# Routing tables and expert weights in attention with a top-1 expert layer: limits read from PSUM, weight splits moved, three first products ahead

## The chip, the cores and the metric

The kernel runs on one core of a Trainium2 chip. The metric is the device time of one execution in microseconds (us). A core has TensorE (matrix products into PSUM), VectorE, ScalarE, GpSimd and SyncE (SP, which here only issues DMAs); the profile calls them PE, DVE, ACT, POOL and SP. PEld is TensorE's loading of weights. Line numbers (L681) are those of the kernel before.

## What is computed

The reference takes q, k and v of 8 batches, 8 heads, 576 rows and 64 columns, and does thresholded attention followed by a layer of 8 experts of which each token uses one:

```python
scores = scale * np.matmul(q, k.transpose(0, 1, 3, 2))
thresh = np.max(scores, axis=-1, keepdims=True) - tau
scores = np.where(scores >= thresh, scores, -1000000000.0)
attn = softmax(scores)                       # over the last axis
x = (attn @ v) laid out as 4608 tokens x 512
expert_idx = np.argmax(x @ w_gate, axis=1)   # gate_w: its softmax probability
for e in range(8):
    mask = expert_idx == e
    h = np.maximum(x[mask] @ w1[e], 0.0)     # 512 -> 1024
    out[mask] = gate_w[mask, None] * (h @ w2[e])
```

All in float32. The kernel keeps that precision by splitting each value into a high and a low float16 half and adding three products (high by high, high by low, low by high).

## The kernel before

**Order of the work.** The kernel is written as a list of steps k. A pair is two heads; there are 32 pairs (NPAIR) of 11 steps each (NSTEP), four pairs to a batch. In the step loop (L1178 to L1211) a pair's scores are made first to find row maxima (`s_unit`, L345), then, ten steps later, made again transposed with the threshold subtracted (`st_unit`, L398): ScalarE takes the exponential (L421), VectorE the mask (L424), ScalarE casts to float16 (L429, the high half) and GpSimd subtracts (L430, the low half; two pieces of the last pair are VectorE's). `av_piece` (L447) multiplies both halves with v, for which `split_v` (L282) and `low_part` (L248) prepare v's halves: ScalarE casts, TensorE puts the cast into a PSUM bank with an identity product (L254), VectorE subtracts (L255). Other work is put into steps with `plan(k, f)` and `after(k, f)`; `hurry(f)` runs f, and all that f plans, with preference. KEND = 352 is the step at which the last pair's scores are done.

Within the emitted program a scheduler orders each engine's instructions by readiness in its own timing model, earlier emitted ones first. `keep_in_program_order` pins an instruction behind what was emitted before it on its engine, and preference ranks it ahead. Each engine, and each DMA queue, then runs its list in order.

**Routing.** When a batch's attention is done, `finish` (L504) scales it, sends the rows through SP's transposes (L543), and `logits` (L551) and `route` (L576) pick each token's expert and its place. `send` (L632) scatters the rows with GpSimd's indirect DMA to one DRAM area per expert (`xs`). Tables of row numbers are made three times, after batches 5, 6 and 7 (`tables0`, `tables1`, `tables2`, L1036 to L1051, through `level`, L1007): `counts` (L661) sums the tokens per expert on TensorE into a PSUM bank and subtracts each expert's base (L665) into the SBUF tile cnt; `table_first` (L668) makes lim = cnt - 1 (L681) and has = cnt > 0.5 (L689), both SBUF to SBUF, then the rows and the flags of rows past the limit, in the same PSUM bank (L682 to L691), and casts them to integers (L658). From table 0 the tiles 0 to 2 of expert 0 are gathered (`fetch`, L819: GpSimd indirect DMA L847, SP transpose L857, small operations L860 and L865), from table 1 tiles 3 to 6, from table 2 the others. A tile is 128 tokens.

**Experts.** `gemm1` (L878) multiplies a group's tokens with w1 on TensorE (L902), ScalarE and VectorE make the two halves of relu (L890, L891); `gemm2` (L914) multiplies with w2 (L935), ScalarE scales by the gate (L946), GpSimd scatters to the output (L949). Groups 0 to 7 are single tiles. `experts` (L1058) gives the order: first product of group i, then second product of group i - 1. Both come in chunks of 12 x 128 columns. Up to step 336 none is emitted, then 0.15 chunk a step, from 352 one chunk a step.

**Weights.** `load_w` (L786) loads a 512 KB quarter of w1 or w2 through SP, `split_w` (L801) makes its halves: ScalarE casts (L806), for expert 0 with the identity product and VectorE's subtraction (L255), pinned in program order, for others VectorE subtracts directly (L814). Expert 0 has two load buffers. Its eight splits, w1 then w2, stand at steps 318, 320, ..., 332 (L1085 to L1088), with the loads two ahead of them. The other experts' weights are due at chunks; 'close' (L1076) at step 364 opens their eight buffers.

Of the kernel before, what the change touches and what calls it, by code (L numbers as in the profile page):

```python
# [14 lines left out]
ALU = mybir.AluOpType  # L15
# [3 lines left out]
B, H, S, D = 8, 8, 576, 64  # L19
# [31 lines left out]
def kernel(  # L51
# [123 lines left out]
    def plan(k, f, where=END):  # L175
        if urgent[0]:
            f = hurry(f)
        assert (k, where) >= (now[0], slot[0])
        acts.setdefault(k, ([], [], []))[where].append(f)

    def hurry(f):

        def g():
            was, urgent[0] = urgent[0], True
            with tc.high_priority():
                f()
            urgent[0] = was

        return g
# [471 lines left out]
    def counts(nm):  # L661
        pc = ps_m.tile([P, 512], F32, tag="m", name=f"pc_{nm}")
        nc.tensor.matmul(pc[:, 0:E], ones, run, start=True, stop=True)
        c = tp.tile([P, E], F32, name=f"cnt_{nm}")
        nc.vector.tensor_tensor(c, pc[:, 0:E], base_e, ALU.subtract)  # L665
        return c, pc

    def table_first(nm, bank, cnt, start=None):  # L668

        bc = [P, E, NE]  # L670
        if start is None:
            rk_i = tp.tile(bc, I32, name="rk_i")
            nc.gpsimd.iota(rk_i, pattern=[[0, E], [P, NE]], base=0, channel_multiplier=1)
            nc.vector.tensor_copy(rk_f, rk_i)
        rk, bad = (bank[:, z:z + E * NE].rearrange("p (e n) -> p e n", e=E) for z in (32, 96))
        if start is None:
            nc.scalar.copy(rk, rk_f)
        else:
            nc.vector.tensor_tensor(rk, rk_f, start.unsqueeze(2).to_broadcast(bc), ALU.add)
        lim = tp.tile([P, E, 1], F32, name=f"lim{nm}")  # L680
        nc.vector.tensor_scalar(lim[:, :, 0], cnt, -1.0, None, ALU.add)  # L681
        nc.vector.tensor_tensor(bad, rk, lim.to_broadcast(bc), ALU.is_gt)  # L682
        nc.vector.tensor_scalar(bad, bad, float(1 << 20), None, ALU.mult)
        badi = to_int(bad, bc, f"badi{nm}")
        nc.vector.tensor_tensor(rk, rk, lim.to_broadcast(bc), ALU.min)
        nc.vector.tensor_tensor(rk, rk, base_e.unsqueeze(2).to_broadcast(bc), ALU.add)

        has = tp.tile([P, E, 1], F32, name=f"has{nm}")
        nc.vector.tensor_scalar(has[:, :, 0], cnt, 0.5, None, ALU.is_gt)  # L689
        nc.vector.scalar_tensor_tensor(rk, rk, pos0, has.to_broadcast(bc), ALU.subtract, ALU.mult)  # L690
        nc.vector.tensor_scalar(rk, rk, pos0, None, ALU.add)  # L691
        rowi = to_int(rk, bc, f"row{nm}")
        return rowi, badi
# [76 lines left out]
    groups += [(m, m + 1) for m in range(NPR, NEARLY, 2)]  # L770
    groups += [(m,) for m in range(NEARLY, NS)]
    group_of = {m: (g, i) for g in groups for i, m in enumerate(g)}
    ms = {}
    wq = {}
    T = {}
# [25 lines left out]
    def split_w(e, w, c):  # L801
        wf = wq.pop((e, w, c))

        o = (wb1, wb2)[w][0 if e == "x" else e % 2][:, c].rearrange("p (a h d) -> p a h d", a=w + 1, h=2)
        x = wf.rearrange("p (a d) -> p a d", a=w + 1)
        hi = nc.scalar.activation(o[:, :, 0], x, AF.Copy, scale=SW)  # L806
        if e == 0:
            tc.keep_in_program_order(hi)
            for i in range(2):
                t = slice(512 * i, 512 * i + 512)  # L810
                y = (x[:, i], o[:, i, 0], o[:, i, 1]) if w else (x[:, 0, t], o[:, 0, 0, t], o[:, 0, 1, t])
                after(2, lambda y=y, i=i: low_part(*y, SW, f"w{w}_{c}_{i}"), END if i else MID)
            return
        nc.vector.scalar_tensor_tensor(o[:, :, 1], x, SW, o[:, :, 0], ALU.mult, ALU.subtract)  # L814
# [59 lines left out]
    def chunks(g):  # L874

        return 8 * shape(g)[1] // P
# [180 lines left out]

    def experts():  # L1058

        for i in range(len(groups) + 1):  # L1060
            if i < len(groups):
                assert there(groups[i], 0)
                yield from gemm1(groups[i])
                past[0] = groups[i][-1]
            if i:
                assert there(groups[i - 1], 1)
                yield from gemm2(groups[i - 1])
                past[1] = groups[i - 1][-1]

    def room():  # L1070
        ldp.close()
# [11 lines left out]
    k = NSTEP * (NPAIR - 2) - LEAD - SL  # L1083
    plan(k + 1, room)
    for i in range(8):  # L1085
        plan(k + WS0 + WSD * i, lambda i=i: split_w(*wseq[i]))
        if i + 2 < 8:
            plan(k + WS0 + WSD * i, lambda i=i: load_w(*wseq[i + 2]))  # L1088
    TABLES = {B - 3: tables0, B - 2: tables1, B - 1: tables2}
    plan(KEND + 12, close)  # L1090


# [7 lines left out]

    at = []
    k = 0
    for i, g in enumerate(groups):
        at.append(k)
        k += chunks(g) + (chunks(groups[i - 1]) if i else 0)
    for i, g in enumerate(groups):
        for j, m in enumerate(g):
            if m >= NF + 2:
# [29 lines left out]
    def there(g, w):  # L1138

        e = g[0] // NE if g[0] < NEARLY else E + g[0] - NEARLY  # L1140
        return all((e, w, c) in split_done for c in range(4))
# [149 lines left out]
```

## Time and profile before

| | |
|---|---|
| median of 3 runs | 994.06 us (992.13 to 997.44) |
| profiled execution, its own time | 992.38 us |
| its span, first to last instruction | 990.7 us |
| mean granted TensorE clock | 0.987 of full speed |
| TensorE / VectorE / ScalarE / GpSimd busy | 95% / 71% / 66% / 57% of the span |

The profile is one execution. A timeline row gives the start and duration in us, the engine, the line, the operation, what it writes and reads, the size, a count where like instructions are merged, and in brackets how long the engine stood idle before it and what ended the idle time. A wait for several things is put down to the one that came last. Spans of GpSimd are rough, and ends of matrix products are modelled.

### The profile page before, as it was taken

What the parts mean: (1) busy time and instruction counts of PE and PEld (TensorE: products, weight loads), DVE (VectorE), ACT (ScalarE), POOL (GpSimd) and SP (SyncE); (2) the same over time, 40 slices, a digit from 0 to 9 for tenths busy, and PEclk for the clock granted to TensorE, in tenths of its full rate; (3) what the DMA queues carried; (4) which work ended last, traced back from release to release, by engine and by line L of the source; (5) the groups of instructions that cost most, each with busy time, mean ns of one, the idle gap of its engine ahead of it and who ended that gap; (6) DMA issues with size and microseconds to landing.
All of it is one profiled execution on the core that took longest, in us unless ns stands there. A gap on an engine that the chain in (4) does not pass through costs nothing. (4 is left out here: it accounts for less than half of the span.)

```text
span 990.7 us, 28651 instructions
## 1 busy us (share of the span) xinstructions
PE 939.0 (95%) x11548; PEld 604.1 (61%) x11548; DVE 702.8 (71%) x1413; ACT 652.3 (66%) x1111; POOL 561.6 (57%) x470
## 2 busy tenths in 40 slices
PE   7899999999999999999897898999999999999997
PEld 2355556556566556565564586777667766667684
DVE  7899999998999989999899875826243342423650
ACT  2689897997998889898988973534243342433651
POOL 6366886895996987978968871433122121221121
PEclk8899999999999999999999999999999999999999
DMA  6553554564564755646646639998574656556730
GB/s 199 143 132 80 146 134 125 140 164 112 127 179 115 162 125 141 171 94 170 152 97 188 149 104 289 363 228 250 164 232 115 216 151 180 171 155 209 224 105 27
DMA packets 142750, 159.20 MB, mean 161 GB/s; under 512 B 96403, under 2 KB 112789, under 8 KB 142614
## 3 DMA queue, kind: packets, MB, share of 16 engines
q1 hardware_dynamic: 126598, 100.33, 40.2%
q10 hardware_dynamic: 6768, 27.55, 8.9%
q0 software_dynamic: 9248, 29.45, 8.9%
q8 instruction: 92, 1.51, 0.7%
q14 instruction: 44, 0.36, 0.1%
HBM read 90.24 MB, written 19.44 MB: 111 GB/s over the span
## 5 line engine op out<-in xcount | busy, mean ns | idle before, releaser
L430 POOL TENSOR_TENSOR pl<-e,ph 128x1024 f16<-128x1024 f32 x158 | 335.9, 2134 | 105.1 <-ACT ph L429 66.6
L421 ACT ACTIVATE e<-st,ntau 128x512 f32<-128x512 f32 (+1 forms) x352 | 222.5, 650 | 54.2 <-PE st L405 51.5
L424 DVE SCALAR_TENSOR_TENSOR e<-st,e 128x512 f32<-128x512 f32 (+1 forms) x352 | 219.7, 635 | 12.2 <-ACT e L421 11.4
L935 PE MATMUL y<-wb,hl 128*128 128x512 f16 (+1 forms) x1056 | 201.8, 360 | 0.0
L368 DVE TENSOR_REDUCE nm<-s 128x1 f32<-128x512 f32 x300 | 188.1, 632 | 19.1 <-PE s L358 16.8
L902 PEld LDWEIGHTS <-wb 128*128 128x128 f16 x2304 | 188.2, 98 | 19.8 <-issue 1.2
L902 PE MATMUL h<-xTm,wb 128*128 128x256 f16 (+2 forms) x2112 | 195.2, 253 | 0.7 <-DMA xTm<-R 0.7
L474 PE MATMUL av<-vop,ph 128*128 128x65 f16 (+3 forms) x3072 | 187.7, 195 | 2.3 <-ACT x L484 2.0
L474 PEld LDWEIGHTS <-ph 128*128 128x128 f16 (+1 forms) x3072 | 158.3, 100 | 46.3 <-issue 21.3
L474 PE MATMUL av<-vop,pl 128*128 128x65 f16 (+1 forms) x1536 | 167.5, 194 | 4.6 <-POOL pl L430 4.5
L429 ACT CAST ph<-e 128x1024 f16<-128x1024 f32 x160 | 166.2, 1040 | 5.3 <-DVE e L424 5.0
L474 PEld LDWEIGHTS <-pl 128*128 128x128 f16 (+1 forms) x1536 | 136.6, 100 | 35.8 <-issue 10.5
L935 PEld LDWEIGHTS <-hl 128*128 128x128 f16 (+1 forms) x1056 | 94.0, 100 | 97.9 <-issue 1.9
L814 DVE SCALAR_TENSOR_TENSOR wb<-wf,wb 128x1024 f16<-128x1024 f32 x88 | 103.9, 1220 | 52.0 <-ACT wb L806 51.9
L404 PE MATMUL st<-QK 128*128 128x512 f16 (+3 forms) x640 | 138.8, 294 | 1.9 <-DVE lo L255 0.8
L405 PE MATMUL st<-CQ,ck 128*128 128x512 f16 (+3 forms) x640 | 137.4, 288 | 0.0
L356 PE MATMUL s<-QK 128*128 128x512 f16 (+1 forms) x600 | 129.6, 293 | 3.1 <-DMA QK<-hi 2.0
L358 PE MATMUL s<-ck,CQ 128*128 128x512 f16 (+1 forms) x600 | 128.0, 289 | 1.2 <-DMA CQ<-hi 1.2
L949 POOL DMA_INDIRECT out_dram<-o,gt x40 | 46.6, 1165 | 129.9 <-ACT o L946 118.8
L890 ACT ACTIVATE hl<-h 128x512 f16<-128x512 f32 (+1 forms) x80 | 45.6, 572 | 105.6 <-PE h L902 103.6
L806 ACT ACTIVATE wb<-wf 128x1024 f16<-128x1024 f32 x96 | 97.4, 1049 | 26.9 <-DMA wf<-in_w_dram 10.7
L860 DVE COPY gt<-R 128x1 f32<-128x1 f32 x33 | 5.1, 153 | 129.0 <-DMA out_dram<-o,gt 105.8
(194 smaller groups left out, 1016.6 us busy)
## 6 DMA issues: line engine op xcount, KB each, us to landing
wf<-in_w_dram SPq DMA_DIRECT2D x96, 512.0 KB
qkf<-in_qk_dram ACTq DMA_DIRECT2D x30, 576.0 KB
vf<-in_v_dram ACTq DMA_DIRECT2D x15, 640.0 KB
QK<-hi SPq DMA_DIRECT2D x64, 144.0 KB
QK<-lo SPq DMA_DIRECT2D x64, 72.0 KB
QK<-hi SPq DMA_DIRECT2D x64, 72.0 KB
ck<-lo SPq DMA_DIRECT2D x64, 72.0 KB
CQ<-hi SPq DMA_DIRECT2D x64, 64.0 KB
```

Of the source, the lines that this page charges most:

```text
L356: nc.tensor.matmul(sc[rows, oc], d["QA"][a][:, cols], d["KB"][a][:, CH[c]], start=True, stop=False)
L358: nc.tensor.matmul(sc[rows, oc], d["CQ"][:, at:at + cols.stop - cols.start], d["CK"][a][:, CH[c]], start=False, stop=True,)
L368: nc.vector.tensor_reduce(o, sc[:, 0:width(t)], axis=AX.X, op=ALU.max, negate=True)
L404: nc.tensor.matmul(sc[rows, oc], d["KB"][a][:, cols], d["QA"][a][:, CH[c]], start=True, stop=False)
L405: nc.tensor.matmul(sc[rows, oc], d["CK"][a][:, cols], d["CQ"][:, q], start=False, stop=True)
L421: nc.scalar.activation(pf, sc, AF.Exp, bias=ntau, scale=0.125 / SS)
L424: nc.vector.scalar_tensor_tensor(pf, sc, 0.0, pf, ALU.is_ge, ALU.mult)
L429: nc.scalar.copy(h, pd)
L430: (nc.vector if (n, t) in PLV else nc.gpsimd).tensor_tensor(l, pd, h, ALU.subtract)
L474: nc.tensor.matmul(av[:, 0:D] if z == 2 else av, l if z == 1 else h, vop[:, tv, W:W + D] if z == 2 else vop[:, tv, 0:W], start=i in (0, NT ...
L902: nc.tensor.matmul(o, Wt[:, c, wh, f], x, start=c == 0 and z == 0, stop=c == 3 and z == 2,)
L935: nc.tensor.matmul(o, h[:, hh], Wt[:, f, wh, c], start=f == 0 and z == 0, stop=f == 7 and z == 2)
```

## The change

`counts` writes the difference into the PSUM bank and copies it to SBUF with ScalarE; `table_first` reads the limit and the test from the bank. `experts` follows a list of turns, in which the first product of group 2 comes ahead of the second product of group 0; after that the order is as before. Expert 0's splits of w2 move from steps 326, 328, 330 and 332 to steps 353, 355, 357 and 359, those of w2 are no longer pinned in program order, and the loads of the last two quarters of w2 move along from steps 326 and 328 to 353 and 355. `tables0` is emitted with preference, and with it the gathers of tiles 0 to 2. The due chunks of later gathers follow from the new list (only group 5's differs, 25 instead of 33).

```diff
@@ counts
-        nc.vector.tensor_tensor(c, pc[:, 0:E], base_e, ALU.subtract)
+        nc.vector.tensor_tensor(pc[:, 8:8 + E], pc[:, 0:E], base_e, ALU.subtract)
+        nc.scalar.copy(c, pc[:, 8:8 + E])
@@ table_first
-        nc.vector.tensor_scalar(lim[:, :, 0], cnt, -1.0, None, ALU.add)
+        nc.vector.tensor_scalar(lim[:, :, 0], bank[:, 8:8 + E], -1.0, None, ALU.add)
...
-        nc.vector.tensor_scalar(has[:, :, 0], cnt, 0.5, None, ALU.is_gt)
+        nc.vector.tensor_scalar(has[:, :, 0], bank[:, 8:8 + E], 0.5, None, ALU.is_gt)
@@ after group_of
+    turns = [(1, 0), (1, 1), (1, 2), (0, 0), (0, 1), (1, 3), (0, 2)]
+    turns += [(w, i + w) for i in range(3, len(groups)) for w in (1, 0) if i + w < len(groups)]
@@ split_w
-        if e == 0:
+        if e == 0 and w == 0:
             tc.keep_in_program_order(hi)
...
@@ experts
-        for i in range(len(groups) + 1):
-            if i < len(groups):
-                assert there(groups[i], 0)
-                yield from gemm1(groups[i])
-                past[0] = groups[i][-1]
-            if i:
-                assert there(groups[i - 1], 1)
-                yield from gemm2(groups[i - 1])
-                past[1] = groups[i - 1][-1]
+        for first, i in turns:
+            assert there(groups[i], 1 - first)
+            yield from (gemm1 if first else gemm2)(groups[i])
+            past[1 - first] = groups[i][-1]
@@ the splits of expert 0
     for i in range(8):
-        plan(k + WS0 + WSD * i, lambda i=i: split_w(*wseq[i]))
+        t = k + WS0 + WSD * i if i < 4 else KEND + 1 + 2 * (i - 4)
+        plan(t, lambda i=i: split_w(*wseq[i]))
         if i + 2 < 8:
-            plan(k + WS0 + WSD * i, lambda i=i: load_w(*wseq[i + 2]))
-    TABLES = {B - 3: tables0, B - 2: tables1, B - 1: tables2}
+            plan(t, lambda i=i: load_w(*wseq[i + 2]))
+    TABLES = {B - 3: hurry(tables0), B - 2: tables1, B - 1: tables2}
@@ due chunks of the gathers
-    for i, g in enumerate(groups):
-        at.append(k)
-        k += chunks(g) + (chunks(groups[i - 1]) if i else 0)
+    for begin, i in turns:
+        if begin:
+            at.append(k)
+        k += chunks(groups[i])
```

## Rows read from the trace of the kernel before

**Rows 1.** Busy us by stretch: PE, PEld, DVE, ACT, POOL, then PEclk, DMA share, GB/s.
```profile
536.80:541.80 5.00, 1.02 (x6) 0.29 (x3) 5.00 (x5) 2.52 (x4) 4.83 (x4) 1.00 0.93 232
541.80:546.20 4.40, 4.36 (x13) 1.12 (x14) 4.40 (x10) 2.54 (x4) 2.72 (x4) 0.61 0.40 103
546.20:558.00 11.80, 7.38 (x103) 4.70 (x103) 10.73 (x26) 11.10 (x17) 11.11 (x8) 1.00 0.74 197
558.00:588.00 30.00, 30.00 (x686) 25.55 (x683) 21.90 (x57) 24.51 (x53) 22.69 (x18) 1.00 0.37 86
588.00:655.00 67.00, 63.45 (x748) 45.13 (x746) 43.66 (x113) 29.57 (x46) 24.23 (x26) 1.00 1.06 302
...
541.80:583.20 41.40, 36.94 (x671) 26.67 (x672) 33.63 (x76) 36.46 (x64) 35.54 (x28) 0.96 0.49 120
```

**Rows 2.** Timeline of VectorE: limit and test of table 0, limit of table 1.
```profile
536.80 4.29 DVE L681 TENSOR_SCALAR lim<-cnt 128x8 f32<-128x8 f32 x1
541.01 0.16 DVE L689 TENSOR_SCALAR has<-cnt 128x8 f32<-128x8 f32 x1
...
583.55 0.17 DVE L681 TENSOR_SCALAR lim<-cnt 128x8 f32<-128x8 f32 x1
...
584.89 0.20 DVE L683 TENSOR_SCALAR pc<-pc 128x32 f32<-128x32 f32 x1
```

**Rows 3.** Timeline of GpSimd at the same time.
```profile
536.71 2.28 POOL L536 TENSOR_TENSOR R<-xn,R 128x512 f16<-128x512 f32 x2
538.94 2.12 POOL L430 TENSOR_TENSOR pl<-e,ph 128x1024 f16<-128x1024 f32 x1
```

**Rows 4.** Timeline of TensorE, 537 to 558 us: its waits, and two like products.
```profile
537.44 0.38 PE L358 MATMUL s<-ck,CQ 128*128 128x512 f16 x1
541.82 0.77 PE L254 MATMUL hi_w<-wb,ident_h 128*128 128x512 f16 x2 [4.00 <-DVE nm L368]
...
543.84 0.63 PE L358 MATMUL s<-ck,CQ 128*128 128x512 f16 x1
...
550.42 0.59 PE L254 MATMUL hi_w<-wb,ident_h 128*128 128x512 f16 x2 [1.41 <-ACT wb L806]
...
553.57 0.59 PE L254 MATMUL hi_w<-wb,ident_h 128*128 128x512 f16 x2 [0.63 <-ACT wb L806]
...
557.41 0.44 PE L254 MATMUL hi_v<-vop,ident_h 128*128 128x320 f16 x2 [2.27 <-ACT vop L286]
```

**Rows 5.** ScalarE's groups, 543 to 581 us; one copy; the low halves' minimum/median/maximum (ns).
```profile
L421 ACT ACTIVATE e<-st,ntau 128x512 f32<-128x512 f32 (+1 forms) x25 | 15.5, 661 | 4.3 <-PE st L405 4.2
...
L806 ACT ACTIVATE wb<-wf 128x1024 f16<-128x1024 f32 x4 | 4.2, 1049 | 0.1
...
583.61 0.17 ACT L1020 COPY pc<-cnt 128x8 f32<-128x8 f32 x1 [0.89 <-DVE cnt L665]
...
L255 DVE SCALAR_TENSOR_TENSOR wb<-wf,hi_w x16: 665/675/687, 528.1 to 559.4; 128x512 f16<-128x512 f32 x16
```

**Rows 6.** GpSimd's groups, 541 to 583.3 us, and its last low half.
```profile
L430 POOL TENSOR_TENSOR pl<-e,ph 128x1024 f16<-128x1024 f32 x12 | 25.6, 2133 | 3.1 <-ACT ph L429 3.0
L633 POOL DMA_INDIRECT xs<-R,posi x4 | 4.3, 1071 | 0.8 <-issue 0.8
L847 POOL DMA_INDIRECT Rm<-xs,row x3 | 3.0, 983 | 1.9 <-DVE e L424 1.4 <-issue 0.3 <-PE av L474 0.2
...
581.04 2.13 POOL L430 TENSOR_TENSOR pl<-e,ph 128x1024 f16<-128x1024 f32 x1
```

**Rows 7.** Waits from 560 to 660 us (total, times, longest): ScalarE's for weights, SP's for gathers.
```profile
ACT wb L806 <- DMA wf<-in_w_dram: 10.1, 6, 3.7
...
SPq L857 <- DMA Rm<-xs,row: 4.1, 2, 3.7
```

**Rows 8.** Timeline of TensorE: a tile's first product, and tile 7's.
```profile
621.85 5.52 PE L902 MATMUL h<-spare,wb 128*128 128x128 f16 x96
...
654.81 5.52 PE L902 MATMUL h<-xTm,wb 128*128 128x128 f16 x96 [0.74 <-DMA xTm<-R]
```

## Prediction

> **What bounds the kernel now.** I read the page's busy shares first, then the busy time by stretches, then the timelines of the engines around the stretch that stands out. By stretches [rows 1], TensorE is all but gapless from 558 us on (30.00 of 30 us, 63.45 of 67), so whatever brings the work of this second part forward shortens the run, provided that its inputs come forward too. Just ahead of it lie three poor stretches: 1.02 busy of 5.0 us, then 4.4 us at a mean granted clock of 0.61, then 7.38 of 11.8.
>
> The cause of the first is one VectorE instruction. The limit of the first table, 128x8, takes 4.29 us at 536.80, while the same line takes 0.17 us at 583.55 [rows 2]. On GpSimd element-wise work runs back to back over just that time, from 536.71 to 541.06, and VectorE's next one starts at 541.01 [rows 2, 3]: VectorE waits until GpSimd falls free. TensorE waits 4.00 us behind it for a score bank, and a 512-column product then takes 0.63 us where it took 0.38 before: by the mean clock of 0.61 most of that stretch runs at 1.2 GHz instead of 2.4 [rows 1, 4]. The third stretch is ScalarE's: TensorE waits 1.41 and 0.63 us for splits of the second weights and 2.27 us for the split of v, which stands behind one of them on ScalarE [rows 4]; four such splits take 4.2 us there [rows 5].
>
> A rule of the Trainium skill bears on the first (SBUF — State Buffer, Who interferes with whom): a VectorE tensor_scalar with both ends in SBUF can take the port pair that it shares with GpSimd, the later of the two blocks until the first finishes, and a PSUM operand rules that mode out. The trace agrees on the block, not on its length: by the rule it ends with one GpSimd instruction, by the rows it lasted until GpSimd had none left, 4.29 us. If one instruction were the limit, the first term below would be about half.
>
> **The change part by part.** The sum is made against the profiled execution, 992.38 us; the median of the runs shown is 994.06, so 1.68 us is added at the end.
>
> *Limits from PSUM.* Subtraction, limit and test stay three small VectorE instructions per table. For a scalar operation that reads PSUM the nearest row is the table's own one of 0.20 us [rows 2]. That takes 4.1 us off VectorE, once; the other tables have nothing to lose. On TensorE it gives back the 4.00 us and, for the half-speed stretch, 4.4 x (1 - 0.61) = 1.7 us. A copy of 128x8 on ScalarE comes in three times, 0.17 us by the nearest copy [rows 5]. Bounds: nothing, or, in the last table, up to 3.7 us behind a weight split that waits for its load [rows 7]. I take nothing, since the limit no longer reads the copied value.
>
> *Second weights behind the last pair.* Four ScalarE splits (4.2 us), eight VectorE low halves of 0.68 us [rows 5], eight 512-column products and two 512 KB loads leave the time from 544 to 560 us. TensorE's three waits, 4.3 us, go at most. The work comes back some 20 to 30 us later, where ScalarE is busy 24.51 of 30 us and DMA only to 0.37 [rows 1]. Its cost there is between nothing, where ScalarE fills its idle time, and 3.7 us a split, the longest wait of one for its load [rows 7], with the exponentials and evacuations of the last pair queued behind it. I take nothing, because the row of DMA at 0.37 is the nearer one: the 3.7 us was seen at 1.06. On VectorE the low halves (8 x 0.68 = 5.4 us) stand ahead of the last batch's scaling at worst; 21.90 of 30 us are busy there. SP issues the two late loads as buffers fall free, ahead of the last batch's transposes, and passes none of them.
>
> *Three first products ahead.* The third tile's 96 products, 5.52 us a tile [rows 8], pass the first tile's second ones. The work is the same; TensorE gets 24 chunks of cover instead of 16 while the second weights arrive. Should that cover end early, the price is the wait above and a low clock after it. The gather of tile 5 comes due eight chunks sooner, at no cost: table 1 has its rows by then, and the next product to need it is as far off as before.
>
> *First table preferred.* Some twelve VectorE instructions of about 0.2 us come sooner, and with them three gathers, three SP transposes and the small copies on VectorE and GpSimd. No product waits for these tiles now, so nothing is gained. The gathers (0.98 us each) pass low halves on GpSimd, and one of them already stops that queue for 1.4 us [rows 6]: bounds 1.4 us gained and twice that lost. On SP the transposes can wait 3.7 us for gathered rows [rows 7], ahead of the last pair's thresholds; they stand there today too, so nothing.
>
> **The sum.** TensorE alone would come forward by 4.00 + 1.7 + 1.41 + 0.63 + 2.27 = 10.0 us. But the second part needs the last batch, and that needs the last pair's low halves from GpSimd. From 541.8 to 583.2 us GpSimd is busy 35.54 of 41.4; only ScalarE has more, 36.46, and it is to lose 4.2 [rows 1]. Of GpSimd's idle time 3.0 us stand ahead of low halves and 1.4 ahead of a gather; the rest are gaps of some 0.2 us ahead of gathers and sends [rows 6]. So its last low half, at 581.04, can come 4.4 us sooner. Three of the four sends of this stretch stand late, among the last low halves; at (4.3 + 0.8) / 4 = 1.3 us each they are another 3.8 us if all fall behind the last low half: 8.2. ScalarE allows 4.2 us of waits for TensorE and 4.2 of splits, 8.4 [rows 5]. I take the middle of 4.4 and 8.2, 6.3 us, because the sends' own inputs come forward as well, so that some will stay ahead. From there the last batch's chain is as before up to tile 7, for which TensorE already waits 0.74 us at 654.81 [rows 8]. So the chain hands its 6.3 us to the end, and what TensorE has beyond, 3.7 us, turns into a longer wait for that tile or for the last logits. 992.38 - 6.3 + 1.68 = 987.8 us, and 985.9 to 989.7 between the two ends.
>
> **The rivals.** *GpSimd is no limit*: all its sends move behind, and the last batch's chain shortens where it stands behind weight splits. Then the full 10.0 us, 984.1. For it: those splits wait 10.1 us for loads, in six waits [rows 7]. Against: the 0.74 us at tile 7 says that the chain is the last to come.
>
> *The splits come back.* They are no longer pinned in ScalarE's order, which is otherwise made by readiness, and only two of their loads are late; the first two could run among the last pairs as before. Then that part of the change does not do what it says: the lock goes, ScalarE keeps 2 to 4 us, and GpSimd gains 2 to 3 of its 4.4 us: 991.5. Against: ScalarE has little room there, 36.46 of 41.4.
>
> *A new stop on GpSimd.* The preferred gathers wait at the head of its queue for the last scatter or for a buffer, and its 1.4 us become 4.2: 4.4 - 2.8 = 1.6 us of gain, 992.5. For it: the same wait today. Against: the low halves have eight buffers, which can cover it.
>
> *Slower: the second weights come late.* Their last two loads need buffers that the first two splits free, so ScalarE meets them one by one. If each of the four splits waits 3.7 us, with the last pair's evacuations behind, the chain grows by 14.8 and gains 6.3: 8.5 us, 1002.6. It decides from 6.3 / 4 = 1.6 us a split. Against it stands DMA's low share there.
>
> **How the numbers follow.** 0.5% is 5.0 us, about what a measurement of this kernel can tell from no change. Chances: forecast 0.55, GpSimd no limit 0.12, splits come back 0.15, new stop 0.10, slower 0.08. Of the forecast's span of 4.4 to 8.2 us of gain some five sixths lie above 5.0, 0.47; with the 0.12 that is 0.59 for faster. The rest of the forecast and the two small gains make 0.33 within 0.5%, and 0.08 is slower. The range runs from a little below the full gain to a little above the new stop, 983.0 to 993.0, and leaves out the slower case and the edges of the others.
>
> **What would show it.** Right: the limit's line near 0.2 us three times; no wait of 4 us on TensorE near 540 and a clock of 1.00 there; no split of the second weights before the last exponentials are nearly done; GpSimd's last low half starting near 575; TensorE gapless up to a wait of some us at the last logits or at tile 7. Wrong: the 4 us wait again behind another instruction, so that the block was not the limit's own; second-weight splits among the last pairs' exponentials; ScalarE idle for a weight load with an evacuation behind it; a low clock at the first second products.

## The result, and the profile after

The changed kernel takes 1003.02 us (median, 1000.04 to 1006.02) against 993.84 us before: ratio 1.009, 95% interval 1.0065 to 1.0115. Slower by 9.2 us, where 6.3 us less were forecast.

From which point on do the two traces differ? The first 256-column product of group 8, the first group of two tiles, starts at 664.91 before and here:

```profile
675.70 1.04 PE L905 MATMUL h<-xTm,wb 128*128 128x256 f16 x8
```

That is 325.8 us ahead of the span's end in both (990.7 and 1001.5), and 325.7 to 326.0 in 17 of the 20 traces of this study (in the other three the work stands in another order there). From that product on nothing of the change matters. The busy time by stretches up to it (columns as in [rows 1]), first of the kernel before, then of the changed one:

```profile
480.00:560.00 80.00, 68.35 (x1041) 41.11 (x1038) 73.31 (x153) 67.74 (x120) 66.47 (x47) 0.98 0.57 150
560.00:600.00 40.00, 39.10 (x790) 32.52 (x789) 29.59 (x72) 28.80 (x60) 27.45 (x24) 1.00 0.55 119
600.00:664.91 64.91, 62.26 (x729) 44.50 (x730) 34.95 (x98) 28.60 (x40) 22.58 (x24) 1.00 1.07 310
```

```profile
480.00:560.00 80.00, 65.44 (x1037) 40.96 (x1036) 75.45 (x143) 66.11 (x118) 63.38 (x43) 0.94 0.57 140
560.00:600.00 40.00, 35.20 (x735) 29.53 (x736) 25.50 (x65) 28.54 (x60) 29.57 (x24) 1.00 0.43 101
600.00:675.70 75.70, 70.61 (x781) 48.45 (x782) 45.91 (x115) 31.49 (x46) 28.60 (x31) 0.98 1.03 292
```

TensorE's idle time (length less PE busy) grows by 2.9, 3.9 and 2.4 us in the three; with 0.3 less ahead of 480 us that is 8.9 of the 10.8 us. The rest is busy time, at a mean granted clock of 0.94 instead of 0.98 in the first. Of the idle time, 2.4 us behind 599 us stand in front of products that wait for nothing that the profile shows (it calls this "issue"); the kernel before has none of it, and set E comes back to it. The first 2.9 us begin on VectorE. Its timeline, the answer to [rows 2]:

```profile
539.52 0.15 DVE L682 TENSOR_SCALAR lim<-pc 128x8 f32<-128x8 f32 x1
...
542.20 9.05 DVE L817 SCALAR_TENSOR_TENSOR wb<-wf,wb 128x1024 f16<-128x1024 f32 x1
...
554.48 1.21 DVE L817 SCALAR_TENSOR_TENSOR wb<-wf,wb 128x1024 f16<-128x1024 f32 x1
...
557.69 1.88 DVE L817 SCALAR_TENSOR_TENSOR wb<-wf,wb 128x1024 f16<-128x1024 f32 x1
...
560.26 0.19 DVE L658 CAST row<-pc 128x32 int32<-128x32 f32 x1
560.86 1.78 DVE L817 SCALAR_TENSOR_TENSOR wb<-wf,wb 128x1024 f16<-128x1024 f32 x1 [0.40 <-ACT wb L809]
```

The limit now takes 0.15 us where it took 4.29. But four operations stand there that the kernel before has not in this place: the second weights' low halves, 128x1024, made directly from the load and from the high half, both in SBUF. One takes 9.05 us; the 92 of this line have a median of 1.22. GpSimd at that time, the answer to [rows 3]:

```profile
541.73 2.04 POOL L528 TENSOR_TENSOR xn<-x,rs 128x512 f32<-128x512 f32 x2
543.73 4.20 POOL L430 TENSOR_TENSOR pl<-e,ph 128x1024 f16<-128x1024 f32 x2
547.90 2.26 POOL L536 TENSOR_TENSOR R<-xn,R 128x512 f16<-128x512 f32 x2
556.35 5.20 POOL L430 TENSOR_TENSOR pl<-e,ph 128x1024 f16<-128x1024 f32 x2 [6.19 <-ACT ph L429]
...
589.67 2.14 POOL L430 TENSOR_TENSOR pl<-e,ph 128x1024 f16<-128x1024 f32 x1
```

Its work is back to back until 550.16, and VectorE's operation ends at 551.25, 1.09 us later: about one undisturbed run of it, begun when GpSimd fell free. Then GpSimd itself is idle for 6.19 us, since ScalarE and TensorE are stuck behind VectorE, and its last low half starts at 589.67, where it was 581.04 [rows 6]. TensorE's waits, the answer to [rows 4]:

```profile
551.89 0.59 PE L404 MATMUL st<-QK 128*128 128x512 f16 x1 [7.92 <-DVE nm L368]
...
571.52 1.29 PE L905 MATMUL h<-xTm,wb 128*128 128x128 f16 x20 [1.41 <-DMA xTm<-Rm]
...
613.39 0.46 PE L561 MATMUL lg<-wg,xTg 128*128 128x8 f16 x12 [3.18 <-DMA xTg<-R]
```

Behind the 7.92 us come the later ones. Table 0's rows are cast at 560.26 (553.18 before), so a first product waits for its gathered tile at 571.52; the last batch is late as a whole, and its logits wait for transposes. ScalarE's high halves were planned behind the last pair, whose last exponential starts at 583.6. It ran the first here:

```profile
541.11 1.06 ACT L809 ACTIVATE wb<-wf 128x1024 f16<-128x1024 f32 x1 [1.39 <-DMA wf<-in_w_dram]
```

and at 546.18, 556.17 and 559.77. Without the pin the scheduler draws them forward to where they are ready, and VectorE's low halves with them.

### The profile page after: what moved, and what is told of

Its sections match the earlier page's. It is cut to its first block, busy times and chain, and to the rows that moved or that the text cites. A ratio compares the mean times of both kernels' runs of the same rounds, so it can differ in the third digit from the quotient of the medians.

```text
span 1001.5 us, 28637 instructions
## 1 busy us (share of the span) xinstructions
PE 940.9 (94%) x11540; PEld 604.8 (60%) x11540; DVE 707.9 (71%) x1409; ACT 653.3 (65%) x1114; POOL 563.1 (56%) x470
## 5 line engine op out<-in xcount | busy, mean ns | idle before, releaser
L817 DVE SCALAR_TENSOR_TENSOR wb<-wf,wb 128x1024 f16<-128x1024 f32 x92 | 117.9, 1318 | 53.6 <-ACT wb L809 48.6
L952 POOL DMA_INDIRECT out_dram<-o,gt x40 | 44.5, 1112 | 137.1 <-ACT o L949 126.2
L949 ACT ACTIVATE o<-y,gt 128x512 f32<-128x512 f32 (+1 forms) x40 | 26.6, 664 | 95.5 <-PE y L938 74.3
```

## The experiments

Each set of runs was on one chip, beside its own runs of the kernel before. This matters: one program gave 0.9963 in set B and 1.0049 in set E, another 1.0034 in C and 1.0116 in E. So ratios are compared within a set; across sets I use only what differs by more than 0.9%, or what the traces show. (A and C were on the same chip, but their traces differ in one thing that set E comes to.) The changed kernel's 1.0090 is a set of its own.

### Set A: two parts alone, two kinds of pin

**limits_alone**, the kernel before with the limits from PSUM (first two hunks of the diff) and nothing else.

> The kernel before with one part of the change: subtraction, limit and test through the PSUM bank, the rest as before. If the block of 4.29 us was the shared-port wait of an instruction that had both ends in SBUF (theory 1), the limit of table 0 takes about 0.2 us, no TensorE wait of 4 us is left near 540, and 4 to 8 us are gained: about 986 to 990. If the time of the stretch is set by GpSimd's work whatever VectorE waits for (theory 2), the instruction is short and the time stays within 2 us of before.

995.49 us, 1.0016 (0.9995 to 1.0037). The limit is down to 0.15 us, and 4.0 us of TensorE's wait become 1.9. GpSimd's last low half starts at 581.08, as before. GpSimd's queue stood still for table 0's third gather, and the last logits for a transpose:

```profile
563.63 0.97 POOL L848 DMA_INDIRECT Rm<-xs,row  x1 [3.37 <-DVE lg L598]
```

```profile
599.32 0.46 PE L561 MATMUL lg<-wg,xTg 128*128 128x8 f16 x12 [2.85 <-DMA xTg<-R]
```

Both waits are shorter before (1.4 us at the gather [rows 6], at most 0.6 at the logits). Alone, the removed stall is worth nothing at the end.

**direct_alone**, the kernel before with the low halves of the changed one:

```diff
-        if e == 0:
+        if e == 0 and w == 0:
```

> The kernel before with one line changed: split_w's condition is e == 0 and w == 0, so the second weights of expert 0 take the direct low half and lose the pin, at the old steps. Theory 1: one or more of the four direct low halves takes 3 to 9 us beside GpSimd's work, and the time is 3 to 10 us over before, with the 4.29 us of the limit still there or merged into the same wait. Theory 3: no slower than before by over 2 us.

999.06 us, 1.0056 (1.0034 to 1.0079). One condition, in the kernel before, makes it slower: shown. (It takes the pin and the low half's form together.) Three of the four low halves meet GpSimd and take 2.74, 2.07 and 2.94 us, and the limit's wait (4.28 us) stays beside them.

**pinned_identity**, the changed kernel with pin and identity product for both weights:

```diff
-        if e == 0 and w == 0:
+        if e == 0:
```

> The changed kernel, but with split_w's condition as before (e == 0): the first expert's second weights keep the low halves by identity product and stay pinned, so they run behind the last pair. Theory 1 (the loss is VectorE's direct low halves with two SBUF inputs, which wait for GpSimd): no VectorE instruction of 9 us, the TensorE wait of 7.9 us gone, 983 to 990. Theory 3 (the loss comes from the rest: preferred tables, the order of turns, late weights): still about 1000.

1002.2 us, 1.0066 (1.0043 to 1.0089). Here the splits truly stand behind the last pair, as the prediction costed them. GpSimd's last low half starts at 575.58, as forecast, 5.5 us sooner, and still the time is longer. ScalarE's timeline shows what delays table 1 first:

```profile
579.99 1.06 ACT L809 ACTIVATE wb<-wf 128x1024 f16<-128x1024 f32 x1 [2.19 <-DMA wf<-in_w_dram]
580.95 0.16 ACT L1023 COPY pc<-cnt 128x8 f32<-128x8 f32 x1
582.28 1.06 ACT L809 ACTIVATE wb<-wf 128x1024 f16<-128x1024 f32 x1 [1.17 <-DMA wf<-in_w_dram]
583.25 0.15 ACT L1030 COPY s_e<-pc 128x8 f32<-128x8 f32 x1
```

Table 1's small copies stand behind weight splits that wait for their loads; VectorE waits 3.55 us for the first. The larger part comes on VectorE itself: from 581.14, where that wait ends, the table's operations take 14.4 us to the cast of the rows, where the like stretch before takes 3.9 us (583.81 to 587.69), because the second weights' low halves, the last batch's scaling and halves of relu stand between them. Its rows are cast at 595.52 (587.69 before), and GpSimd, with nothing else to do, waits 17.11 us for them:

```profile
595.97 1.19 POOL L850 DMA_INDIRECT spare<-xs,row  x1 [17.11 <-DVE row L658]
```

How much of the loss this is, is not shown: TensorE's longest waits behind 590 us are 3.43 and 1.72 us for transposes of the last batch, and 4.6 us are stops of the kind "issue".

**pinned_direct**, the changed kernel with the second weights' high halves pinned, low halves direct.

```diff
+        if e == 0:
             tc.keep_in_program_order(hi)
```

> The changed kernel, with the second weights' splits pinned in order again but their low halves made directly by VectorE from two SBUF inputs, as in the changed kernel. They then run behind the last pair, where GpSimd has less to do. Theory 1 with place: each of the four direct low halves costs 1.2 us plus what GpSimd still has running, at most 2 to 4 us, and the time is within 4 us of the identity version. If the direct form itself is slow wherever it stands, it loses 8 us or more against it.

1002.74 us, 1.0087 (1.0059 to 1.0116), not to be told from the kernel above: behind the last pair, where GpSimd has little left, the form of the low half counts for little (3.60 us is the longest), and what the two share counts, the late place beside the other parts of the change.

### Set B: three more parts alone, and the low halves taken back

**turns_alone**: the kernel before with the list `turns` and the loop over it.

> The kernel before with the new order of the experts' products alone: first products of groups 0, 1 and 2, then the second products of 0 and 1, first product of 3, second of 2, and from there in turn. Limits, second weights, their pin and their low halves as before. Theory 1 (queues: what stands ahead of the last batch, table 1 and table 2 on ScalarE, VectorE and SyncE decides, not the order of TensorE's products): same time, 992 to 996 us, ratio 0.998 to 1.002, and from group 8's first product to the end again 325.8 us. Theory 2 (the order itself is a loss of its own: tiles 3 and 4 are wanted earlier, so that TensorE stands in front of them, and the tables' copies and evacuations come in another order): 997 to 1001 us, ratio 1.003 to 1.007, with a wait of TensorE on a transposed tile of slot 3 or 4 of over 2 us that the kernel before doesn't have.

996.5 us, 1.0029 (1.0009 to 1.0049), a small loss of its own, without the wait that theory 2 named: TensorE's longest behind 580 us is 2.69, for VectorE's count of the last batch. Its cause is open.

**hurry_alone**: `B - 3: hurry(tables0)` in the kernel before.

> The kernel before with the first tables emitted with preference, and nothing else. Theory 1 (queues): the first tables' row is ready somewhat sooner than 553.2 us, the last batches' work behind it moves by no more than 1 us, time 993 to 996 us, ratio 0.999 to 1.002. Theory 3 (preference pushes the last pair's and the last batches' operations on VectorE back, and what the first tables gain the last batch loses): last low half after 582 us, table 2's row after 637 us, time 996 to 999 us, ratio 1.002 to 1.005.

990.59 us, 0.998 (0.9954 to 1.0006): no difference that can be told; table 0's rows are cast at 547.4 and the last low half starts at 577.1, so nothing was pushed back.

**late_splits_alone**: the second weights' steps 353 to 359 in the kernel before, pin and identity product kept.

> The kernel before with the four second-weight splits behind the last pair and nothing else: order of the products, limits, pin and low halves through the identity product as before. Theory 1 (queues: the splits stand ahead of table 1 and the last batch on ScalarE, and the later weight loads on SyncE's queue follow them): slower, 998 to 1002 us, ratio 1.004 to 1.008; the last low half about 5 us sooner than 581.0, but table 1's row after 592 us and table 2's after 639 us, and splits on ScalarE that wait over 1 us for their DMA behind 575 us. Theory 2 (it is the order of the products that loses in the pinned kernels): no slower than before, 988 to 994 us, ratio 0.994 to 1.000, with table 2's row no later than 636 us.

998.06 us, 1.0033 (1.001 to 1.0057): a loss, as theory 1 said, though neither the last low half (581.7) nor table 1's rows (579.8) stand where it said; table 2's are late (638.2 against 635.9).

**identity_unpinned**, the changed kernel with one thing taken back, the low halves' form:

```diff
-        if e == 0 and w == 0:
-            tc.keep_in_program_order(hi)
+        if e == 0:
+            if w == 0:
+                tc.keep_in_program_order(hi)
```

> The changed kernel with the second weights' low halves through the identity product again (two halves, GpSimd and VectorE from PSUM, as the kernel before has them), the high halves still unpinned. If the direct low halves are what loses (theory of two SBUF inputs beside GpSimd): VectorE has no operation of 9 us near 542, TensorE's wait of 7.92 us at 551.89 is under 4 us, the last low half is back to 578 to 582 us, time 993 to 998 us, ratio 0.999 to 1.004. If the place of the splits or the order of the products loses by itself, as in the kernel with pin and identity (1.0066): 999 to 1003 us, ratio 1.005 to 1.009, although that wait is gone.

990.33 us, 0.9963 (0.9941 to 0.9984): faster than before, and than both expectations, and 12.7 us below the changed kernel's median (3.6 us by set E, where it ran again; the changed kernel ran in neither set). In its trace VectorE has no long operation near 542, and no wait of TensorE from 540 to 560 passes 2 us:

```profile
543.27 0.20 PE L474 MATMUL av<-vop,ph 128*128 128x65 f16 x1 [1.77 <-ACT ph L429]
549.62 0.28 PE L379 MATMUL pst<-ident,r 128*9 128x128 f32 x1 [0.68 <-DVE row L658]
551.83 0.21 PE L474 MATMUL av<-vop,ph 128*128 128x65 f16 x1 [1.94 <-ACT x L484]
```

Two of the four splits still run among the last pairs here (541.23 and 546.30), two behind them (581.52 and 585.01), and GpSimd's last low half starts at 579.69.

### Set C: where the low halves stand, and what else is needed

**low_pinned**, the changed kernel with the four direct low halves pinned behind the last pair, ScalarE's part free:

```diff
-        nc.vector.scalar_tensor_tensor(o[:, :, 1], x, SW, ...)
+        low = nc.vector.scalar_tensor_tensor(o[:, :, 1], x, SW, ...)
+        if e == 0:
+            tc.keep_in_program_order(low)
```

> The changed kernel with one thing more: VectorE's four direct low halves of the second weights are pinned to their place in the program, behind the last pair, while ScalarE's high halves may still move. Theory 1 (place: the direct low halves lose because they are drawn in between the last pair's masks and the first tables, beside GpSimd's back-to-back work, where one took 9.05 us): no low half over 4 us, TensorE's wait of 7.92 us near 552 is gone, the first tables' row is back from 560.3 to 553 or sooner, time 988 to 995 us, ratio 0.995 to 1.002. Theory 2 (form: the direct low half loses wherever it stands, or pinned work behind the last pair does, as in the kernel with the direct halves and the high halves pinned, 1.0087): 999 to 1004 us, ratio 1.005 to 1.010, although that wait is gone.

995.19 us, 1.0031 (1.0009 to 1.0053), between the two theories. The wait of 7.92 us is gone and table 0's rows come at 545.0; the longest low half takes 3.59 us. What is left is the late place again: table 1's rows at 595.7, the last logits 6.13 us behind a transpose.

**identity_noturns**, the kernel identity_unpinned with the order of the products as before.

> The changed kernel with the identity product for the second weights' low halves and the order of the products as before: so limits, preference, second weights unpinned and planned behind the last pair. If the order of the products loses by itself here too, as alone (1.0029), this is faster than the same kernel with the new order (0.9963): 985 to 989 us, ratio 0.991 to 0.996. If the new order is what makes room for the late second weights, as the change pairs the two, the time is longer than 990 us: ratio 0.998 to 1.003, with TensorE waiting over 2 us for second weights or for the first products' halves.

992.6 us, 0.9997 (0.9977 to 1.0017), no difference from before. Whether the order of the products helps or loses here stays open, since the 0.9963 is of another set; TensorE's longest wait behind 560 us, 4.45 us, is for a transpose of the last batch and not for second weights.

**identity_nolimits**, the kernel identity_unpinned with the limits from SBUF.

> The changed kernel with the identity product for the second weights' low halves and the tables' limits reading SBUF as before. If the limits' stall of 4.29 us on VectorE is paid at the end, as the prediction had it, this is 3 to 5 us slower than the same kernel with limits from PSUM (0.9963): 993 to 996 us, ratio 1.000 to 1.003. If the stall is off the path, as the kernel with the limits alone has it (1.0016): 988 to 992 us, ratio 0.994 to 0.998, although the limit takes over 2 us again.

996.48 us, 1.0034 (1.0018 to 1.005), just above the first expectation. The limit waits again, and TensorE 4.00 us behind it.

**unpin_hurry**, the kernel before with preference and without the second weights' pin (identity product kept).

> The kernel before with two of the change's parts: first tables with preference, and the second weights' high halves no longer pinned (low halves through the identity product, planned where they were). No limits from PSUM, no new order, nothing planned behind the last pair. If letting the second weights' splits move and the preference make the gain of the kernel with the identity product (0.9963): 988 to 991 us, ratio 0.994 to 0.998. If the gain needs the later place: 991 to 995 us, ratio 0.997 to 1.002.

990.04 us, 0.9985 (0.9968 to 1.0003): no gain that can be told from none.

### Set D: one low half or three

**first_low_early** and **first_low_late** pin, of the four direct low halves, the last three and only the first:

```diff
+        if e == 0 and c > 0:      # first_low_late: c == 0
+            tc.keep_in_program_order(low)
```

> The changed kernel with VectorE's second, third and fourth direct low halves pinned behind the last pair; the first stays where the changed kernel draws it, ahead of the first tables' limits, where it took 9.05 us. Theory 1 (the one collision with GpSimd carries most of the loss): that low half takes over 7 us again, TensorE waits over 6 us behind it, time 999 to 1003 us, ratio 1.006 to 1.010, against 1.0031 with all four pinned. Theory 2 (the other three, which stand between the first tables' operations and the last masks, carry it): 995 to 997 us, ratio 1.002 to 1.004, although the 9 us are there.

1002.56 us, 1.0086 (1.0057 to 1.0115). With one low half in its old place the kernel loses about as much as the changed one did in its own set, although the other three are away; how much of that is the low half, the kernels beside it at the end of this set say. VectorE and TensorE:

```profile
539.40 8.66 DVE L817 SCALAR_TENSOR_TENSOR wb<-wf,wb 128x1024 f16<-128x1024 f32 x1
```

```profile
548.71 0.58 PE L404 MATMUL st<-QK 128*128 128x512 f16 x1 [7.63 <-DVE nm L368]
```

> The changed kernel with only the first of VectorE's four direct low halves pinned behind the last pair; the other three stay early. Theory 1 (the one collision): no low half over 5 us between 538 and 570, first tables' row ready by 556 us, time 994 to 998 us, ratio 1.001 to 1.005. Theory 2 (the other three in the way of the tables and masks): 1000 to 1004 us, ratio 1.007 to 1.010. If the second low half now meets GpSimd's back-to-back work in its place, a low half of 5 us or more stands in the trace, and the run doesn't tell the two apart.

1010.45 us, 1.016 (1.0119 to 1.02), outside both expectations, by the case that its last sentence left open: with the first away, the second and the third meet GpSimd.

```profile
545.38 5.97 DVE L817 SCALAR_TENSOR_TENSOR wb<-wf,wb 128x1024 f16<-128x1024 f32 x1 [0.60 <-ACT wb L809]
...
556.60 5.36 DVE L817 SCALAR_TENSOR_TENSOR wb<-wf,wb 128x1024 f16<-128x1024 f32 x1 [2.51 <-issue]
```

```profile
548.15 2.11 POOL L430 TENSOR_TENSOR pl<-e,ph 128x1024 f16<-128x1024 f32 x1
...
556.67 4.20 POOL L430 TENSOR_TENSOR pl<-e,ph 128x1024 f16<-128x1024 f32 x2
```

**unpin_hurry_limits** is unpin_hurry with limits from PSUM; **identity_early** is identity_unpinned with the second weights' steps as before.

> The kernel before with limits from PSUM, first tables with preference and the second weights' high halves unpinned; identity product, planned place and order of the products as before. If the limits are worth in company what the pair with and without them showed (0.9963 against 1.0034, 7 us), this gains some 5 us on the same kernel without limits (0.9985): 984 to 988 us, ratio 0.991 to 0.995. If that difference came from how the queues happened to be ordered and not from the limit's wait, as the limits alone (1.0016) have it: 989 to 993 us, ratio 0.997 to 1.001.

999.48 us, 1.0046 (1.0023 to 1.007), slower than both expectations.

> The changed kernel with the identity product for the second weights' low halves, and the second weights planned where the kernel before has them, not behind the last pair; limits, preference, unpinned high halves and new order kept. If the later plan is what gains (it leaves the last two splits behind the last pair): 992 to 996 us, ratio 1.000 to 1.004, with low halves between 544 and 560 us and TensorE waiting over 3 us for ScalarE's halves there. If the plan adds nothing and only delays weights and transposes on SyncE's queue: 986 to 990 us, ratio 0.993 to 0.997, and the last batch's transposes come sooner than with the later plan.

997.91 us, 1.0029 (1.0006 to 1.0052), by the time a little above the first expectation. The low halves run between 544 and 558 us, but TensorE's waits for ScalarE's halves there come to 2.8 us, under the 3 us named.

On this chip four kernels, all with limits from PSUM, preference and ScalarE's part unpinned, lie at 1.0029 and 1.0046 with the identity product, at 1.0086 with one long low half and at 1.016 with two: 0.4 to 0.6% more for the first, 1.1 to 1.3% for both. (They differ in the planned steps, and unpin_hurry_limits in the order of the products too.) unpin_hurry_limits can't be set against unpin_hurry, which ran on another chip.

### Set E: the limits in company, on one chip

**identity_pair** and **nolimits_pair** are identity_unpinned and identity_nolimits again, together.

> The changed kernel with the identity product again (0.9963 in its own comparison), now on one chip with its twin without limits from PSUM. If the 12.6 us between it and the changed kernel are the low half's form, this holds: 988 to 992 us, ratio 0.994 to 0.999. If that comparison was kind to it: ratio 0.999 to 1.004, and the loss through the low half is nearer to 0.6% than to 1.3%.

999.45 us, 1.0049 (1.0027 to 1.0072), a little slower than both expectations.

> The same kernel with the limits from SBUF (1.0034 in its own comparison). If the limits' stall is paid at the end in this company, it is again 0.5 to 0.9% longer than its twin: ratio 1.001 to 1.006. If not, as the limits alone (1.0016) and the pair without the later second weights (0.9985 without, 1.0046 with) have it, the two are within 0.3% of each other or the twin with limits is the longer.

1005.44 us, 1.0116 (1.0093 to 1.014), above both ranges, but 0.7% longer than its twin, as the first expectation had it. Two things follow. In this set the limits from PSUM are worth 6.0 us in the company of the other parts, though nothing alone in set A; whether through the limit's wait is not shown. And the gain that identity_unpinned showed in set B is a loss here, so no version of this study can be said to beat the kernel before in every set.

What makes the difference between sets is open, but one sign of it is in the traces. identity_nolimits and nolimits_pair are one program, each profiled within 1 us of its median. Up to 580 us TensorE is busy for 539.60 and 540.36 us. From there to group 8's first product (columns as in [rows 1]; first identity_nolimits, then nolimits_pair):

```profile
580.00:669.63 89.63, 82.31 (x1034) 59.65 (x1031) 51.81 (x130) 39.34 (x60) 35.72 (x36) 0.98 0.99 273
580.00:678.14 98.14, 87.61 (x1039) 63.78 (x1036) 53.92 (x132) 39.39 (x60) 30.63 (x36) 0.95 0.87 252
```

In the second, TensorE is busy longer, at a granted clock of 0.95 instead of 0.98, and it stops again and again in front of products whose wait the profile cannot name:

```profile
642.02 0.22 PE L905 MATMUL h<-xTm,wb 128*128 128x128 f16 x1 [0.52 <-issue]
642.75 0.22 PE L905 MATMUL h<-xTm,wb 128*128 128x128 f16 x1 [0.51 <-issue]
```

From 480 us to group 8 such stops add up to 7.1 us there and to none in the first. They stand in the trace of the changed kernel (2.4 us) and of every run of sets A, D and E (1.5 to 7.1 us), and in none of sets B and C, nor of the kernel before. A and C were on one chip, so the chip alone does not decide it. The sets with stops have ratios of 1.0016 to 1.016, the others 0.9963 to 1.0034. There is one profile of each run, and no experiment aimed at the stops: what causes them, and how much of the changed kernel's loss is theirs, is not shown.

## Why the prediction was wrong

**The step that failed** is the second part of the sum, where the second weights' low halves were "eight VectorE low halves of 0.68 us" that come back later at no cost. The condition `if e == 0 and w == 0` guards not the pin alone but the whole branch, identity product and return included. I read it as the pin's, and the section on the change above says no more than that. The page's counts show the difference: TensorE has 11540 products instead of 11548, and VectorE's direct line 92 operations instead of 88. So four operations with two SBUF inputs enter the stretch in which GpSimd works back to back, the very thing that the first part of the change takes away for the limit. The prediction's last paragraph named the sign, "the 4 us wait again behind another instruction", but gave it no chance. The low half took 9.05 us, and TensorE waited 7.92 us behind it. That the condition loses by itself is shown by direct_alone (0.56% in set A; it takes the pin away too, but unpin_hurry, without the pin and with the identity product, lost nothing in set C). A single such low half costs 0.4 to 0.6% beside the identity kernels of set D. If the sets may be set side by side, that leaves some 0.3 to 0.5% of the changed kernel's 0.9% open; the order of the products (0.3% alone) and TensorE's stops (set E) are candidates.

A rule of the Trainium skill names this case (SBUF — State Buffer, Who interferes with whom): a VectorE instruction with two SBUF inputs contends with a GpSimd instruction that reads SBUF. The rows agree that it is held up; on its length they differ, as they did for the limit (last section).

**The splits come back** was a rival, at 0.15. It is what happened on ScalarE: 541.11 to 559.77 us, all four. Its price, a smaller gain, was worked out for identity products; with direct low halves it is the way by which the loss came in. That the rival of late second weights ended at 1002.6 us, next to the measured 1003.02, is chance: no split of theirs was late in the changed kernel.

**Limits from PSUM.** The mechanism was right: 0.15, 0.17 and 0.15 us in the three tables, no wait behind them. The credit was not as simple as the sum had it: nothing alone (1.0016), 6.0 us in company (set E). One of its terms fails. The 1.7 us for the half-speed stretch did not come back. From 536 to 564 us the granted clock (third column from the end) is not 1.00 in limits_alone and in identity_unpinned but lower than before; it falls there behind waits of 1.93 us (to 540.96) and 1.77 us (to 543.27):

```profile
536.00:564.00 28.00, 19.56 (x260) 10.84 (x257) 26.73 (x55) 22.93 (x39) 24.00 (x20) 0.94 0.73 174
536.00:564.00 28.00, 22.29 (x307) 12.99 (x307) 22.52 (x58) 23.27 (x41) 22.07 (x19) 0.88 0.83 161
536.00:564.00 28.00, 22.96 (x293) 14.14 (x292) 19.97 (x52) 22.89 (x41) 26.54 (x23) 0.76 0.61 136
```

These are before, limits_alone and identity_unpinned. And the last table's way from its counts to its rows, which the sum left as it was, grew longer. In limits_alone the copy of the counts, taken at nothing, comes 4.2 us after the subtraction, behind weight splits. The limit now stands among the operations on the bank, 13.4 us after the subtraction instead of 0.2. The rows are cast 22.2 us after it instead of 18.9; TensorE did not wait for them in that trace.

**GpSimd as the limit, and the chain behind it.** With the splits pinned late, the last low half starts at 575.58; forecast was near 575. The next sentence fails: "the last batch's chain is as before up to tile 7". In pinned_identity the late splits stand in ScalarE's queue ahead of table 1's copies and wait for loads that SP could issue only as buffers fell free. VectorE, with the late low halves in its own queue, then takes 14.4 us for that table. This is the rival with late second weights, given 0.08. Its price, 3.7 us a split, was too high (2.19 and 1.17 are the waits seen there), but it was charged to the evacuations; of the next table's copies the sum had only the new one, at nothing, and not those that VectorE waited for, nor its own queue. I had costed it at nothing because DMA stood at 0.37. That looked at the wrong thing: by SP's waits from 560 to 600 us (total, times, longest) the loads could not be issued before a buffer fell free,

```profile
SPq L794 <- DVE wb L255: 11.1, 2, 10.2
```

and a load issued late is waited for although DMA has room (0.66 from 576 to 583.5 us).

**Three first products ahead** was costed at nothing and has a loss of 2.9 us alone (0.9 to 4.9 by the interval); a small miss, unexplained. **First table preferred** at nothing was right within its interval.

**The size, with the branch as I had read it**: identity_unpinned is the change so read, 990.3 us in set B, inside the range, and 999.5 in set E, outside. Where it was inside, that is luck in part: two of the four splits stayed among the last pairs, and the last low half came at 579.69, not near 575. The range had no room for differences between sets. (Two slips change nothing: five sixths of 0.55 are 0.46, not 0.47, and from 541.8 to 583.2 us TensorE too, with 36.94 of 41.4, was busier than GpSimd.)

## What to carry to other kernels

When a condition is narrowed, list every statement that it guards, and hold the counts of the page against that list. A VectorE operation with two SBUF inputs, put beside GpSimd's back-to-back work, can cost the whole stretch that is left of that work (9.05 us instead of 1.22); with one input from PSUM it didn't (0.69 us at most for half the columns [rows 5]), even with a TensorE product more. And an unpinned operation goes where the scheduler finds it ready, so a step number is no place: read each engine's order in the trace.

## What the runs showed of the hardware

VectorE's wait beside GpSimd need not end with one GpSimd instruction: it can last through a row of them. In the six kernels with direct low halves, fifteen of these that the runs stretched (1.78 to 9.05 us instead of 1.22) end 1.08 or 1.09 us after the end of an element-wise GpSimd instruction: 551.25 against 550.16 here, 548.06 against 546.97 in first_low_early. The 9.05 us span the whole row. Behind twelve of these ends GpSimd has a gap of at least 0.09 us. But in the changed kernel VectorE also got in twice between low halves of GpSimd that follow within 0.04 us (at 558.48 and 561.55), and once in first_low_late (at 560.87), so the row's end is not the whole rule; what lets VectorE in is open. The wait is mutual: two GpSimd low halves that meet such an operation take 5.20 us at 556.35 in the changed kernel, 4.20 elsewhere. The second surprise is the sets: a ratio with an interval of 0.2% either way in one set was 0.8 to 0.9% off in another, for two programs alike (0.9963 to 1.0049, 1.0034 to 1.0116), while the kernel before differed by 0.1 to 0.2% (993.12, 992.26 and 994.14 us in sets B, C and E).
